# A gated feed-forward kernel: the crossbar copy of x rows 256-511 moves to second place on SyncE's queue, and the first weight slices to ScalarE's

## The chip, the cores and the metric

The kernel runs on one core of one Trainium2 chip. The metric is the device time of one execution in microseconds. The kernel before has a median of 163.7 us over three runs (163.27 to 163.84). A profiled execution, taken apart from these, is where durations and order come from.

## The reference

The kernel computes `(silu(x @ w_gate) * (x @ w_up)) @ w_down` in bf16:

```python
B, S, D, F = 1, 2048, 640, 1536
g = _silu(x @ w_gate)          # x: B, S, D   w_gate: D, F
u = x @ w_up                   # w_up: D, F
return (g * u) @ w_down        # w_down: F, D
```

D is five pieces of 128 rows, F is twelve, S is four blocks of 512 rows.

## The kernel before, in words

TensorE multiplies a stationary tile (loaded by a weight load, shown as PEld) with a moving tile of up to 512 columns and adds up in PSUM. For the first two products the moving tile is x transposed, with D on the partitions: the array `xT`. For each of the four blocks of 512 rows of x and each of the twelve pieces of F, five matmuls over D give the gate sum `pg` and five more the up sum `pu` (line 193). ScalarE applies Silu (line 214), VectorE multiplies (line 215) and writes `aT`. Then twelve matmuls over F for each output tile make the third product (lines 261 and 290), and the outputs are copied and stored. The last four rows of x are computed on VectorE in the gaps (`row_dots`, line 147); the change does not touch them.

`xT` is made in two ways. Rows 0 to 255 are loaded as they are (`x_sb`, line 86, two loads of 128 rows, one by SyncE, one by ScalarE) and transposed by TensorE: five transposes for each 128 rows into PSUM (line 185), the first two into a tile `po_a`, the other three into `po_b`, and a copy of each tile into `xT` (line 190; ScalarE copies `po_a`, VectorE `po_b`). Rows 256 to 511 and all others come by a DMA that transposes on its way, through the crossbar (`turn_x`, line 105). The function is called at line 118 for rows 256 to 511.

Loads go out on two queues in the order of the program. SyncE's queue (SP in the profile) has x rows 0-127, then the gate slices for D pieces 0, 2 and 4 (line 115; each is 128 rows of D by the first 512 columns of F, 128 KB), then the crossbar copy of x rows 256-511, then the up weights for the first four F pieces (line 83, two loads), then the remaining weights, further crossbar copies, and later the outputs. ScalarE's queue (ACT) has x rows 128-255, then the gate slices for D pieces 1 and 3; after that ScalarE loads its function table and runs one tiny Silu (line 119).

`head()` (from line 219) writes the order of TensorE's work by hand, up to the first four F pieces of the first block; `keep_order` holds the instructions of an engine to the order written. First 18 small matmuls on ones (`warm`, line 176) that need no load, then the transposes of x rows 0-127 and 128-255, and then the gate sums of four F pieces side by side (`EARLY = 4`), each in its own PSUM tile of 512 columns. The list `steps` sets the order: for D piece 0 columns 0-127, then 128-255; for D pieces 1 to 4 columns 0-255; then for all five D pieces columns 256-511, which need the crossbar copy. Each step is four matmuls, one for each F piece, so 44 in all. Then follow the up sums of the same four F pieces with 512 columns at once, and the regular loop.

The flag `start` of a matmul makes it overwrite what stood in the tile instead of adding. The kernel before sets it for D piece 0 at column 0 and again at column 256.

Of the kernel before, what the change touches and what calls it, by code (L numbers as in the profile page):

```python
# [10 lines left out]
def _body(  # L11
# [8 lines left out]
    nc = tc.nc  # L20
# [12 lines left out]
    KD = D // P  # L33
    KF = F // P
    S_BLK = 512
    NSB = S // S_BLK
    SUB = S_BLK // P
    HALF = S_BLK // 2
# [3 lines left out]
    T = 4  # L42
    WT_STEP = 4
    ROW_J = 0
    EARLY = 4
    W_CHUNKS = [(4, 8), (8, 12)]
    assert D % P == 0 and F % P == 0 and S % S_BLK == 0 and D > DA and SUB == 4

# [30 lines left out]
    def wslice(a, b):  # L79
        return slice(a * P, b * P)  # L80

    def load_w(eng, dst, src, a, b):
        eng.dma_start(out=dst[:, :, wslice(a, b)], in_=src[:, :, wslice(a, b)])

    def load_x(eng, c0, c1):
        eng.dma_start(out=x_sb[:, c0:c1, :], in_=x_v[:, c0:c1, :])
# [11 lines left out]
    def keep_order(engine):  # L98

        traced = [i for i in nc.cur_bb.bb.instructions if i.engine == engine]  # L100
        for a, b in zip(traced, traced[1:]):
            issue_order(a, b)

    def turn_x(r0, r1):
        nc.sync.dma_start_transpose(out=xT[:, :, r0:r1], in_=xt_v[r0:r1])
# [4 lines left out]

    load_x(nc.sync, 0, 1)
    load_x(nc.scalar, 1, 2)
    for kd in range(KD):
        eng = (nc.sync, nc.scalar)[kd % 2]
        eng.dma_start(
            out=wg_sb[:, kd, wslice(0, EARLY)], in_=wg_v[:, kd, wslice(0, EARLY)]
        )
    turn_x(HALF, S_BLK)
    nc.scalar.activation(silu_first[:], ones[:, 0:1], ACT.Silu)  # L119
    for a in range(0, EARLY, 2):  # L120
        load_w(nc.sync, wu_sb, wu_v, a, a + 2)
# [52 lines left out]
    def warm(n):  # L174
        for _ in range(n):
            nc.tensor.matmul(  # L176
                pw[:, 0:P], lhsT=ones[:], rhs=ones[:], start=True, stop=True
            )

    def transpose_chunk(c, parts):  # L180
        c_sl = slice(c * P, (c + 1) * P)
        for copy, tag, k0, k1 in parts:
            pt = psum.tile([P, k1 - k0, P], bf16, tag=tag, name="pt")
            for kd in range(k0, k1):
                nc.tensor.transpose(  # L185
                    out=pt[:, kd - k0, :],
                    in_=x_sb[:, c, kd * P : (kd + 1) * P],
                    identity=ident[:],
                )
            copy(out=xT[:, k0:k1, c_sl], in_=pt[:])  # L190

    def proj_step(ps, w_sb, fc, sb, c0, c1, kd):
        nc.tensor.matmul(  # L193
            ps[:, c0:c1],
            lhsT=w_sb[:, kd, fc * P : (fc + 1) * P],
            rhs=xT[:, kd, sb * S_BLK + c0 : sb * S_BLK + c1],
            start=(kd == 0 and c0 in (0, HALF)),
            stop=(kd == KD - 1),
        )

    def proj(ps, w_sb, fc, sb, c0, c1):
        for kd in range(KD):
            proj_step(ps, w_sb, fc, sb, c0, c1, kd)
# [6 lines left out]
    def gate(pg, pu, sb, fc, n_s):  # L210

        s0 = sb * S_BLK
        sg = work.tile([P, S_BLK], f32, name="sg")
        nc.scalar.activation(sg[:, 0:n_s], pg[:, 0:n_s], ACT.Silu)  # L214
        nc.vector.tensor_tensor(  # L215
            out=aT[:, fc, s0 : s0 + n_s], in0=sg[:, 0:n_s], in1=pu[:, 0:n_s], op=ALU.mult
        )

    def head():
        dve, act = nc.vector.tensor_copy, nc.scalar.copy  # L220
        split = [(act, "po_a", 0, 2), (dve, "po_b", 2, KD)]
        pgs = [
            psum.tile([P, S_BLK], f32, tag="gu", name="pg", bufs=4)
            for _ in range(EARLY)
        ]
        warm(N_WARM)
        for c in range(HALF // P):
            transpose_chunk(c, split)

        steps = [(0, 0, P), (0, P, HALF)]  # L230
        steps += [(kd, 0, HALF) for kd in range(1, KD)]
        steps += [(kd, HALF, S_BLK) for kd in range(KD)]
        for kd, c0, c1 in steps:
            for fc in range(EARLY):
                proj_step(pgs[fc], wg_sb, fc, 0, c0, c1, kd)

        for fc in range(EARLY):
            pu = psum.tile([P, S_BLK], f32, tag=("po_a", "po_b")[fc % 2], name="pu")
            proj(pu, wu_sb, fc, 0, 0, S_BLK)
            gate(pgs[fc], pu, 0, fc, S_BLK)  # L240
        keep_order(mybir.EngineType.PE)
        keep_order(mybir.EngineType.Activation)

    head()
    for sb in range(NSB):
        n_s = S_BLK if sb < NSB - 1 else S_BLK - T
        for fc in range(KF):
            if sb == 0 and fc < EARLY:
                continue
# [10 lines left out]
        for kf in range(KF):  # L260
# [4 lines left out]
                start=(kf == 0),  # L265
# [15 lines left out]
        for j in range(SUB):  # L281
# [5 lines left out]
            for c0, c1, tag in cols:  # L287
                po = psum.tile([P, c1 - c0], f32, tag=tag, name="po_a")
                for kf in range(KF):
# [4 lines left out]
                        start=(kf == 0),  # L294
# [3 lines left out]
                if c1 < D:  # L298
                    nc.scalar.copy(ot[:], po[:])  # L299
                    eng = nc.sync  # L300
                else:
                    nc.vector.tensor_copy(out=ot[:], in_=po[:])  # L302
                    eng = nc.scalar
# [81 lines left out]
def kernel(tc, *args):  # L385
    _body(tc, *args)
    tc.close()
    tc.compile()
    _trim(tc.nc)
# [30 lines left out]
```

## Time and profile before

| What | Value |
|---|---|
| Three timed runs | 163.27, 163.7 (median), 163.84 us |
| Profiled execution | 163.03 us, of it the span from first to last instruction 161.7 us |
| TensorE matmul busy | 158.7 us, 784 instructions |
| Weight loads busy | 77.7 us, 796 instructions |
| VectorE busy | 110.9 us |
| ScalarE busy | 42.5 us |
| Gate sums, line 193 | 258 matmuls, 59.6 us |
| Up sums, line 193 | 239 matmuls, 59.0 us |
| Third product, lines 290 and 261 | 42.4 and 10.3 us |
| Crossbar copy of x rows 256-511 | issued at 1.86 us, 2.13 us of issuing, landed 4.4 us after its start |

Busy times of matmuls overlap one another, because they are pipelined: the distance between two starts says more than the duration of one. A DMA has two times: how long the queue's engine works at issuing it, and how long it takes from the start of the issue until its data has landed. The second is what an engine that waits for the data sees.

### The profile page before, as it was taken

The numbers are of one execution on the slowest core, as the hardware profiler recorded it, in microseconds if no ns is written. First come the engines' busy times: TensorE is split into PE (matmuls) and PEld (weight loads), VectorE is DVE, ScalarE is ACT, GpSimd is POOL, SyncE is SP. The second block draws the span as 40 slices with busy tenths as digits, with TensorE's granted clock in tenths as the row PEclk, the third lists the DMA queues.
The fourth block names the chain that finished last, engine by engine and source line by source line (L and its number), as shares of the span: only waits on it lengthen the run. The fifth ranks groups of instructions, "written<-read, shape, count | busy, mean of one in ns | idle before, by whom it ended". The sixth has DMA issues, their size and how long they took to land.

```text
span 161.7 us, 2102 instructions
## 1 busy us (share of the span) xinstructions
PE 158.7 (98%) x784; PEld 77.7 (48%) x796; DVE 110.9 (69%) x249; ACT 42.5 (26%) x74; POOL 0.6 (0%) x6
## 2 busy tenths in 40 slices
PE   9999999999999999999999999999999999999995
PEld 8854444444444444444444444444444444445464
DVE  2035322599479999889919999979955999993000
ACT  5051222112322222211222322221213222222121
POOL 1000000000000000000000000000000000000000
PEclk9999999999999999999999999999999999999999
DMA  7999999998199993003110000000321000000312
GB/s 230 257 346 353 363 228 209 231 184 135 34 192 167 201 202 84 4 0 38 61 65 0 0 4 2 0 0 6 59 67 34 0 0 0 0 0 4 54 35 73
DMA packets 41817, 15.86 MB, mean 98 GB/s; under 512 B 33232, under 2 KB 41680, under 8 KB 41808
## 3 DMA queue, kind: packets, MB, share of 16 engines
q1 hardware_dynamic: 33296, 14.78, 38.6%
q10 hardware_dynamic: 8512, 0.95, 3.9%
q8 instruction: 6, 0.10, 0.3%
q14 instruction: 3, 0.02, 0.1%
HBM read 6.88 MB, written 2.62 MB: 59 GB/s over the span
## 4 chain that ended last, share of the span: by engine, by line
PE 98%; issue 1%; DVE 0%
PE pg L193 32%; PE pu L193 32%; PE po_a L290 26%; PE po_t L261 6%; PE pw L176 1%; PE pt L185 1%; DVE ot_b L302 0%; DVE ones L109 0%
## 5 line engine op out<-in xcount | busy, mean ns | idle before, releaser
L193 PE MATMUL pg<-xT,wg_sb 128*128 128x512 bf16 (+3 forms) x258 | 59.6, 364 | 0.3
L193 PE MATMUL pu<-xT,wu_sb 128*128 128x512 bf16 (+1 forms) x239 | 59.0, 379 | 0.1
L215 DVE TENSOR_TENSOR aT<-sg,pu 128x512 bf16<-128x512 f32 (+1 forms) x48 | 32.8, 682 | 32.3 <-PE pu L193 32.3
L214 ACT ACTIVATE sg<-pg 128x512 f32<-128x512 f32 (+1 forms) x48 | 28.4, 596 | 70.9 <-PE pg L193 65.6
L290 PE MATMUL po_a<-wd_sb,aT 128*128 128x512 bf16 (+2 forms) x212 | 42.4, 358 | 0.2
L147 DVE SCALAR_TENSOR_TENSOR prod<-wgT,x_row 128x640 f32<-128x640 bf16 x48 | 39.4, 820 | 1.2
L147 DVE SCALAR_TENSOR_TENSOR prod<-wuT,x_row 128x640 f32<-128x640 bf16 x48 | 39.4, 821 | 1.0
L193 PEld LDWEIGHTS <-wg_sb 128*128 128x128 bf16 x264 | 26.1, 100 | 26.5
L193 PEld LDWEIGHTS <-wu_sb 128*128 128x128 bf16 x240 | 23.4, 98 | 28.0
L290 PEld LDWEIGHTS <-aT 128*128 128x128 bf16 x216 | 20.7, 98 | 21.7
L299 ACT CAST ot<-po_a 128x512 bf16<-128x512 f32 (+1 forms) x17 | 9.5, 560 | 32.0 <-PE po_a L290 20.7
L261 PE MATMUL po_t<-aT,wd_sb 128*128 128x512 bf16 (+1 forms) x47 | 10.3, 366 | 0.1
L261 PEld LDWEIGHTS <-wd_sb 128*128 128x128 bf16 x48 | 4.7, 98 | 5.1
L302 DVE CAST ot_b<-po_a 128x128 bf16<-128x128 f32 x1 | 0.3, 290 | 9.9 <-PE po_a L290 9.9
L270 ACT CAST ot_t<-po_t 128x512 bf16<-128x512 f32 (+1 forms) x4 | 2.2, 558 | 11.6 <-PE po_t L261 11.6
L147 DVE DVE_READ_ACCUMULATOR prod<-wuT,x_row 128x1 f32 x48 | 3.9, 82 | 0.0
L147 DVE DVE_READ_ACCUMULATOR prod<-wgT,x_row 128x1 f32 x48 | 3.9, 81 | 0.0
L272 DVE STREAM_TRANSPOSE ot_q<-ot_t 128x512 bf16<-128x512 bf16 (+1 forms) x4 | 2.7, 677 | 1.7 <-ACT ot_t L270 1.7
L190 DVE COPY xT<-pt 128x384 bf16<-128x384 bf16 x2 | 0.7, 356 | 3.0 <-PE pt L185 3.0
L176 PE MATMUL pw<-ones 128*128 128x128 bf16 x18 | 2.1, 313 | 0.4 <-DVE ones L109 0.4
L176 PEld LDWEIGHTS <-ones 128*128 128x128 bf16 x18 | 1.8, 148 | 0.4 <-DVE ones L109 0.4
L119 ACT ACT_TABLE_LOAD x1 | 1.3, 1283 | 1.5 <-issue 1.5
(13 smaller groups left out, 4.6 us busy)
## 6 DMA issues: line engine op xcount, KB each, us to landing
wd_sb<-in_w_down_dram SPq DMA_DIRECT2D x1, 1920.0 KB, 13.7
out_dram<-ot SPq DMA_DIRECT2D x15, 128.0 KB, 1.7
wg_sb<-in_w_gate_dram SPq DMA_DIRECT2D x2, 640.0 KB, 7.4
wu_sb<-in_w_up_dram SPq DMA_DIRECT2D x2, 640.0 KB, 8.4
wu_sb<-in_w_up_dram SPq DMA_DIRECT2D x2, 320.0 KB, 4.4
x_row<-in_x_dram SPq DMA_DIRECT2D x1, 640.0 KB, 5.4
wg_sb<-in_w_gate_dram SPq DMA_DIRECT2D x3, 128.0 KB, 3.7
out_dram<-ot_q ACTq DMA_DIRECT2D x12, 32.0 KB, 1.9
```

The lines of the kernel that those rows point to most:

```text
L119: nc.scalar.activation(silu_first[:], ones[:, 0:1], ACT.Silu)
L147: nc.vector.scalar_tensor_tensor(out=prod[:], in0=wT[:, fc, :], scalar=1.0, in1=x_row[:, t, :], op0=ALU.mult, op1=ALU.mult, accum_out=acc[ ...
L176: nc.tensor.matmul(pw[:, 0:P], lhsT=ones[:], rhs=ones[:], start=True, stop=True)
L185: nc.tensor.transpose(out=pt[:, kd - k0, :], in_=x_sb[:, c, kd * P : (kd + 1) * P], identity=ident[:],)
L193: nc.tensor.matmul(ps[:, c0:c1], lhsT=w_sb[:, kd, fc * P : (fc + 1) * P], rhs=xT[:, kd, sb * S_BLK + c0 : sb * S_BLK + c1], start=(kd == 0 ...
L214: nc.scalar.activation(sg[:, 0:n_s], pg[:, 0:n_s], ACT.Silu)
L215: nc.vector.tensor_tensor(out=aT[:, fc, s0 : s0 + n_s], in0=sg[:, 0:n_s], in1=pu[:, 0:n_s], op=ALU.mult)
L261: nc.tensor.matmul(po_t[:], lhsT=wd_sb[:, kf, DA:D], rhs=aT[:, kf, sb * S_BLK : sb * S_BLK + n_t], start=(kf == 0), stop=(kf == KF - 1),)
L270: nc.scalar.copy(ot_t[:], po_t[:])
L272: nc.vector.transpose(out=ot_q[:], in_=ot_t[:])
L290: nc.tensor.matmul(po[:], lhsT=aT[:, kf, s0 : s0 + P], rhs=wd_sb[:, kf, c0:c1], start=(kf == 0), stop=(kf == KF - 1),)
L299: nc.scalar.copy(ot[:], po[:])
```

## The change

The crossbar copy of x rows 256-511 is issued by SyncE directly after x rows 0-127. The gate slices for D pieces 0, 1 and 2 are issued by ScalarE, those for D pieces 3 and 4 by SyncE, after the crossbar copy. The steps of the head are: D piece 0 in two parts and D pieces 1 and 2 on columns 0-255; D pieces 0, 1, 2 on columns 256-511; D pieces 3 and 4 on all 512 columns. That is 36 matmuls instead of 44, over the same columns. The flag `start` is set at column 0 alone, since a second one at column 256 would fall into the middle of a sum that goes on over all 512 columns. VectorE makes all four copies of transposed tiles; ScalarE makes none.

```diff
-    EARLY = 4
+    EARLY, STEPS = 4, 3
...
     load_x(nc.sync, 0, 1)
     load_x(nc.scalar, 1, 2)
+    turn_x(HALF, S_BLK)
     for kd in range(KD):
-        eng = (nc.sync, nc.scalar)[kd % 2]
+        eng = nc.scalar if kd < STEPS else nc.sync
         eng.dma_start(
             out=wg_sb[:, kd, wslice(0, EARLY)], in_=wg_v[:, kd, wslice(0, EARLY)]
         )
-    turn_x(HALF, S_BLK)
     nc.scalar.activation(silu_first[:], ones[:, 0:1], ACT.Silu)
...
-            start=(kd == 0 and c0 in (0, HALF)),
+            start=(kd == 0 and c0 == 0),
...
-        dve, act = nc.vector.tensor_copy, nc.scalar.copy
-        split = [(act, "po_a", 0, 2), (dve, "po_b", 2, KD)]
+        copy = nc.vector.tensor_copy
+        split = [(copy, "po_a", 0, 2), (copy, "po_b", 2, KD)]
...
         steps = [(0, 0, P), (0, P, HALF)]
-        steps += [(kd, 0, HALF) for kd in range(1, KD)]
-        steps += [(kd, HALF, S_BLK) for kd in range(KD)]
+        steps += [(kd, 0, HALF) for kd in range(1, STEPS)]
+        steps += [(kd, HALF, S_BLK) for kd in range(STEPS)]
+        steps += [(kd, 0, S_BLK) for kd in range(STEPS, KD)]
```

## The prediction

> I name the five weight slices of the first gate matmuls, one per 128-row piece of D, D0 to D4; "the copy" is the crossbar copy of x rows 256-511 (line 105, called at line 118).
>
> **What bounds the kernel now.** First the busy times and the chain of work that ended last, on the page:
>
> ```profile
> PE 158.7 (98%) x784; PEld 77.7 (48%) x796; DVE 110.9 (69%) x249; ACT 42.5 (26%) x74; POOL 0.6 (0%) x6
> ...
> PE 98%; issue 1%; DVE 0%
> ```
>
> TensorE is the whole chain. A change of queues can then gain only where TensorE waits, and lose only where it makes it wait. The diff touches the head, so next comes the chain of the first 14 us, in order of time (start, us, what):
>
> ```profile
> 0.39 2.10 PE pw L176 x18
> 2.50 1.12 PE pt L185 x10
> 3.62 5.14 PE pg L193 x44
> 8.76 0.22 PE pu L193
> ```
>
> Eighteen warm-up matmuls, ten transposes and 44 gate pieces follow each other without a wait. Then the timeline of the same stretch (start, us, engine; the lines with q are a queue's issues):
>
> ```profile
> 0.00 0.39 SPq L86 DMA_DIRECT2D x_sb<-in_x_dram  x1
> 0.13 0.39 ACTq L86 DMA_DIRECT2D x_sb<-in_x_dram  x1
> ...
> 0.45 1.36 SPq L115 DMA_DIRECT2D wg_sb<-in_w_gate_dram  x3
> 0.55 0.93 ACTq L115 DMA_DIRECT2D wg_sb<-in_w_gate_dram  x2
> ...
> 1.51 1.28 ACT L119 ACT_TABLE_LOAD   x1 [1.51 <-issue]
> 1.86 2.13 SPq L105 DMA_TRANSPOSE xT<-in_x_dram  x1
> ...
> 3.30 5.17 PEld L193 LDWEIGHTS <-wg_sb 128*128 128x128 bf16 x44
> 3.41 5.35 PE L193 MATMUL pg<-xT,wg_sb 128*128 128x128 bf16 x44
> ...
> 4.03 1.15 SPq L83 DMA_DIRECT2D wu_sb<-in_w_up_dram  x2
> ```
>
> With the time to landing that the view by source gives for each issue, this makes a table of margins. D0 (SP, 0.45+2.8) lands at 3.25 and its weight load starts at 3.30. D1 (ACT, 0.55+3.5) lands at 4.05, its load starts at 4.16. D2 (SP, 0.91+3.7): 4.6, used at 4.9. D3 (ACT, 1.03+3.8): 4.8, used at 5.43. D4 (SP, 1.38+3.7): 5.05, used at 5.86. The copy (1.86+4.4): 6.25, used at 6.41. Everything arrives just in time and nothing late: there is no stall for the change to remove.
>
> One more thing is read from spacing. The 256-column pieces start 0.21 us apart until 4.90 (at 4.69, then at 4.90), and from 5.10 to 8.59 there are 32 pieces, 0.109 us each. TensorE's clock doubles near 5.08, after 4.7 us without a gap. (The granted-clock column shows 1.00 in every window from 0 on, so it does not show this; the spacing does.)
>
> **The change part by part**, in the time of the profiled execution: span 161.7 us, execution 163.03 us. The three timed runs have a median of 163.7, 0.67 more; I add the difference that I work out to this median.
>
> 1. *Sixteen 256-column pieces (D3, D4) become eight of 512.* At full clock 2 x 0.109 against 0.216 (five pieces of 512 columns in 1.08 us on the chain): 8 x 0.002, a gain of 0.02 us. Pieces that would have run at half clock gain nothing.
>
> 2. *Copies of the transposed chunks, all on VectorE.* Before, ScalarE's two of 128x256 take 0.36 us each and VectorE's two of 128x384 0.36. On VectorE alone the first can start when its transposes end, near 2.8 instead of 2.91, and the four run one after another. A 256-column copy on VectorE is not shown: between 0.24 (0.356 by columns) and 0.36. The third then ends at 3.7 to 3.85, for a piece that starts at 3.83 today; the fourth at 4.1 to 4.2, for D2. Cost 0 to 0.03 us, and 0 if D0 is late (next step). ScalarE must lose these copies, since its third load moves the table load from 1.51 to about 2.0 and its end to 3.3; the next ScalarE work is the Silu at 8.47.
>
> 3. *D0 moves to ScalarE's second place.* This is the step that counts. That place is D1's today: issued at 0.55 behind the same x rows 128-255 on the same queue, landed 3.5 us later. So D0 at 4.05 instead of 3.25, for a load that wants to start at 3.30: a gap of 0.7 to 0.75 us in TensorE. Lower end: it lands as SP's D0 did, 0.55+2.8 = 3.35, a gap of 0.05. Upper end from the only rows where ScalarE's transfers start beside a crossbar copy in flight (stores of line 274; the first answer is for 34 to 37 us, the second for 70 to 160):
>
> ```profile
> DMA to landing us min/median/max: 3.1/3.4/3.5
> ```
>
> ```profile
> DMA to landing us min/median/max: 1.6/1.9/1.9
> ```
>
> Beside the copy of wgT (issued 31.87 to 35.54) they took 1.6 us longer: 4.05+1.6 = 5.65, a gap of 2.3. I take 0.7, the row of the same queue, place and size; there it competes with SP's ordinary loads instead of the copy. [...]
>
> 4. *D1, D2 in ScalarE's third and fourth place.* D1 as today's D3: 1.03+3.8 = 4.8, needed when D0's eight pieces (0.107 each) end at 4.95. D2, issued at about 1.5, as today's D4 by 3.7: 5.2, needed at 5.4 or later. No further gap at the middle; behind the copy they slip with D0.
>
> 5. *The copy as SP's second load.* Issued at 0.45 instead of 1.86: 4.85, needed after D2's first half, 5.9. It is 1 us early where it was 0.16 us early. Nothing is gained, since nothing waited. Its issue holds SP for 2.13 us, so D3 and D4 are issued at about 2.6 and 3.0. By the fastest and the slowest delay of the slices and the copy (2.8, 4.4) they land between 5.4 and 7.4; D3 is needed near 7.2, D4 near 8.05. Line 83's loads go out 0.5 us sooner than at 4.03, because SP issues one load fewer ahead of them, while TensorE is later: every later margin grows.
>
> **What the gap costs.** If the clock still doubles at 5.08, the gap removes 0.7 us of half-clock work, which is made up at full clock: 0.35 us. If the doubling comes later by the gap, 0.7 us. I take the middle, 0.5, with the 0.02 of step 1 inside its rounding. **163.7 + 0.5 = 164.2 us** (163.5 by the profiled execution). Own range of this case: 163.9 to 164.5.
>
> **Rivals.**
>
> A. *No gap.* The copy's packets start late (SP works 2.13 us at issuing it) and leave the 16 engines to ScalarE's queue until then. For: x rows 0-127 are then the only other load ahead of it. Against: step 3's rows. Time 163.6 to 163.9.
>
> B. *The copy shuts ScalarE's queue out.* For: the stores at 34.5. Against: those came when the copy was nearly all issued, D0 comes 0.1 us after its start. Decides if D0 lands after 4.6. Gap 1.3 to 2.3 us, cost 0.65 to 2.3: 164.4 to 166.0.
>
> C. *The gap costs the clock.* The doubling came after 4.7 us of gapless work. If D0's gap starts this count anew at 4.1, the clock doubles at 8.8. Half-clock work from 4.1 to 8.8 is worth 2.35 us at full clock; before did 0.83+3.7 = 4.55 in the same time (from 3.41). Loss 2.2: 165.9. For: the only rise in the trace followed gapless work. Against: a gap of 0.7 in 4.7 leaves TensorE 85% busy, and no row shows what share is needed. [...]
>
> D. *Faster.* If in most executions the clock doubles well before 5.08, before is held by arrivals: an earlier rise could gain it only the 0.16 us that the copy has in hand, while after, with its copy at 4.85, could keep up to 0.5 more. For: the three runs differ by 0.57 us although the program is the same. Against: the profiled execution, the fastest of the four, shows no arrival that held TensorE, so late arrivals are not shown to be what the others lose. It decides if D0 also comes by 3.5. Time 163.2.
>
> **Numbers.** About 0.3% (0.49 us) is what a measurement of this kernel can tell from no change. Forecast 0.40 (0.28 of it over that bound, 0.12 within it), A 0.15, B 0.12, C 0.15, D 0.18 (0.15 over the bound, 0.03 within). Slower 0.28+0.12+0.15 = 0.55, within 0.12+0.15+0.03 = 0.30, faster 0.15. Cases of both signs hold weight, so the range reaches from D's 163.2 to C's 165.9; only B's far end and what lies beyond D are left out.
>
> **What would show it.** Right: TensorE's first weight load of wg_sb near 4.1 with idle time before it that a load ended; D0's time to landing 3.5; the copy landed by 4.9 and nobody waiting for it; spacing 0.109 from about 5.1 to 5.8. A: first gate piece at 3.4. B: D0 to landing over 4.1, x rows 128-255 perhaps late too. C: spacing 0.21 until 8 us. D: fast spacing before 4.5 us. I am wrong in kind if a wait shows at line 83's loads, at D3 or D4, or at a copy on VectorE, which I hold for covered.

## The result, and the profile after

The changed kernel takes 167.79 us (median of six runs, 166.48 to 168.78); the kernel before, beside it, 163.62 us (163.12 to 163.84). The ratio is 1.0254, with a 95% interval of 1.0218 to 1.0291: slower by about 4.2 us, where 0.5 was forecast and 165.9 was the upper end of the range. Each ratio below is to the kernel before timed beside that run (medians of 163.48 to 163.59 us). The ratios of the runs e5, e10 and e11 below leave out executions more than 1.5% above the fastest of their kernel, while their medians hold all.

The profiled execution of the changed kernel took 166.76 us, span 165.4 against 161.7. The up sums of the head start at 12.35 us instead of 8.59, 3.76 us later, and that is the whole difference of the spans. The chain of the first 14 us, which was TensorE alone before (start, us, what):

```profile
...
1.03 5.80 DMA wg_sb<-in_w_gate_dram
6.83 0.05 issue
6.87 5.64 PE pg L193 x28
12.51 1.51 PE pu L193 x7
```

A load is on the chain now: the second of ScalarE's three slices, D1. It is issued at 1.03 and lands 5.8 us later, at 6.83, where step 4 had 3.8. In the timeline, idle time ahead of a row stands in brackets, with what ended it:

```profile
0.46 2.03 SPq L105 DMA_TRANSPOSE xT<-in_x_dram  x1
0.55 1.41 ACTq L116 DMA_DIRECT2D wg_sb<-in_w_gate_dram  x3
...
3.85 0.62 PE L193 MATMUL pg<-xT,wg_sb 128*128 128x128 bf16 x8 [0.34 <-DMA wg_sb<-in_w_gate_dram]
...
6.87 5.64 PE L193 MATMUL pg<-xT,wg_sb 128*128 128x256 bf16 x28 [2.40 <-DMA wg_sb<-in_w_gate_dram]
```

D0's gap is 0.34 us, less than the 0.7 forecast: D0 landed 3.3 us after its issue. The gap that was not forecast is the next one, 2.40 us ahead of D1. The copy of x rows 256-511, which landed 4.4 us after its issue before, now takes 7.0.

A second loss follows from the gap. The view by windows shows the granted clock (the column after POOL); the first three numbers are a stretch's start and end and its length, then comes TensorE's busy time:

```profile
3.27:6.68 3.41, 0.86 (x12) 0.51 (x9) 0.66 (x3) 0.21 (x2) 0.00 (x0) 1.00 1.14 177
6.68:10.09 3.41, 3.22 (x16) 2.30 (x17) 0.00 (x0) 0.00 (x0) 0.00 (x0) 0.50 1.17 306
10.09:12.35 2.26, 2.26 (x15) 1.26 (x13) 0.00 (x0) 0.45 (x1) 0.00 (x0) 1.00 1.10 347
```

Full clock came early, at 3.27 (from there D0's pieces are 0.056 us apart instead of 0.107), was lost at 6.68, with 0.86 us of TensorE work in the 3.41 us between, and was back at 10.09. All work from 6.87 to 10.09 ran at half clock (0.50 in the second line), 3.2 us that would take 1.6 at full clock.

The sum for the profiled execution, from starts of pieces: waits of 0.46 and 2.56, together 3.0; plus 1.6 for the second half-clock stretch; less 0.8, because the kernel before did its gate pieces from 3.41 to 5.08 at half clock, and here the same pieces ran at full clock or are counted in the second half-clock stretch. That makes 3.8, against 3.76 measured.

### The profile page after: what moved, and what is told of

Read it like the earlier page. It is cut to its first block, busy times and chain, and to the rows that moved or that the text cites. A ratio compares the mean times of both kernels' runs of the same rounds, so it can differ in the third digit from the quotient of the medians.

```text
span 165.4 us, 2098 instructions
## 1 busy us (share of the span) xinstructions
PE 160.3 (97%) x788; PEld 77.1 (47%) x788; DVE 111.2 (67%) x251; ACT 41.9 (25%) x72; POOL 0.6 (0%) x6
## 4 chain that ended last, share of the span: by engine, by line
PE 95%; DMA 4%; ACTq 1%; DVE 0%; issue 0%
PE pg L193 32%; PE pu L193 31%; PE po_a L291 25%; PE po_t L262 6%; DMA wg_sb<-in_w_gate_dram 4%; ACTq L116 0%; ACTq L86 0%; DVE ot_b L303 0%
## 5 line engine op out<-in xcount | busy, mean ns | idle before, releaser
L193 PE MATMUL pg<-xT,wg_sb 128*128 128x512 bf16 (+3 forms) x256 | 60.8, 374 | 2.7 <-DMA wg_sb<-in_w_gate_dram 2.7
L193 PEld LDWEIGHTS <-wg_sb 128*128 128x128 bf16 x256 | 25.4, 101 | 30.6 <-DMA wg_sb<-in_w_gate_dram 3.1
L190 DVE COPY xT<-pt 128x256 bf16<-128x256 bf16 (+1 forms) x4 | 1.1, 318 | 2.5 <-PE pt L185 2.5
```

The source lines that it names most:

```text
L193: nc.tensor.matmul(ps[:, c0:c1], lhsT=w_sb[:, kd, fc * P : (fc + 1) * P], rhs=xT[:, kd, sb * S_BLK + c0 : sb * S_BLK + c1], start=(kd == 0 ...
```

## The experiments

Theory M: the crossbar copy and ScalarE's slices, in flight together, slow each other. Rivals: Q, ScalarE's queue is slow by itself; B, any 327 KB in the copy's place make the slices late; S, a copy issued this early is slow by itself; and theory C on how much of the loss is the clock. (B here, any bytes, is not rival B of the prediction, the crossbar copy shutting ScalarE's queue out.)

### e1: the copy behind the slices again

```diff
-    turn_x(HALF, S_BLK)
     for kd in range(KD):
         ...
+    turn_x(HALF, S_BLK)
```

> The changed kernel with the crossbar copy issued by SyncE after D3 and D4 again; queues of the slices, steps and copies as changed. Theory M (mixing: the copy's 256-byte packets and ScalarE's slices slow each other while both are in flight): D0 lands near 3.3 to 3.6, D1 by 4.3, D2 by 4.8, the copy by 6.3 as before; the gap of 2.4 us ahead of D1 goes. A wait of up to 0.9 us for the copy stays, since the new steps want it at 5.4. Time 163.6 to 164.8. Theory Q (ScalarE's queue is slow by itself when it carries three slices behind x rows): D1 still lands after 5.5 and the time stays above 166.

164.57 us, ratio 1.0066 (1.0041 to 1.0092). The gap ahead of D1 is gone, and about three quarters of the loss with it; the copy landed at 6.73. Theory Q falls: D1 landed at 5.19, and the time is far below 166. But M's landing times fail too: D0 landed 4.1 us after its issue, D1 4.2, D2 4.1, so D0 came at 4.6 and not at 3.3 to 3.6. TensorE's longest wait was 0.70 us, for D0:

```profile
4.66 6.41 PE L193 MATMUL pg<-xT,wg_sb 128*128 128x128 bf16 x36 [0.70 <-DMA wg_sb<-in_w_gate_dram]
```

The place of the copy is most of the loss. What is left shows in this profile (of the slowest of the six executions) as the wait for D0, which comes later from its place on ScalarE's queue than from SyncE's (3.25 us in the kernel before). The new steps have a share too, as e6 and e10 below show.

### e2 and e3: no copy, and an ordinary load of the same bytes

```diff
 # e2
-    turn_x(HALF, S_BLK)
+    nc.vector.memset(xT[:, :, HALF:S_BLK], 0.0)
 # e3
-    turn_x(HALF, S_BLK)
+    x_more = consts.tile([P, 2, D], bf16)
+    nc.sync.dma_start(out=x_more[:], in_=x_v[:, 2:4, :])
+    nc.vector.memset(xT[:, :, HALF:S_BLK], 0.0)
```

> The changed kernel without the crossbar copy of x rows 256-511: VectorE fills these columns of xT with zeros, so the outputs of these rows are not computed from x. Theory M, and theory B (any 327 KB ahead of or beside the slices make them late): D0 by 3.5, D1 by 4.1, D2 by 4.6, no gap in TensorE over 0.3 us, time 162.9 to 163.8. Theory Q: D1 after 5.5, time above 166.

> As e2 (x rows 256-511 of xT are zeros), but in the copy's place SyncE issues an ordinary load of the same 327 KB of x (1280-byte rows) that nothing reads. Theory M (the crossbar's packets): D1 lands by 4.7, D2 by 5.2, time 163.0 to 164.2. Theory B (the bytes): D1 lands after 5.5, a gap of over 1.2 us ahead of it, time above 165.5.

e2: 164.94 us, 1.0102 (1.0039 to 1.0165). e3: 165.44 us, 1.0121 (1.0069 to 1.0174). Neither theory was right on both. In e2, without any copy, D1 still landed 4.6 us after its issue, at 5.59, and D2 at 6.54: SyncE's queue, relieved of the copy, put its up loads (320 KB each, the first issued at 1.39) beside ScalarE's slices. So e2 does not remove the competition, it changes it. In e3, D0 to D2 took 4.0, 4.4 and 4.5 us; TensorE waited 0.87 us ahead of D0 and hardly after it. So e3 misses M clearly and B narrowly (D1 landed at 5.46, B had after 5.5 and a gap ahead of it). B's mechanism is real in part: with ordinary bytes in the copy's place the kernel is still 2.0 us slower than before, about half of the loss with the copy. How late they make a single slice is not sharp: D1 takes 4.4 here, 4.2 in e1 and 3.8 in e10, against 5.8 with the copy. What the crossbar adds shows in the DMA view from 3.0 to 5.5 us (packets, MB and mean rate; then the two queues), of the changed kernel

```profile
DMA packets 1080, 0.35 MB, mean 142 GB/s; under 512 B 976, under 2 KB 1080, under 8 KB 1080
...
q1 hardware_dynamic: 966, 0.25, 90.1%
q10 hardware_dynamic: 114, 0.11, 33.3%
```

and of e3:

```profile
DMA packets 1030, 0.88 MB, mean 352 GB/s; under 512 B 96, under 2 KB 1030, under 8 KB 1030
...
q1 hardware_dynamic: 602, 0.49, 61.2%
q10 hardware_dynamic: 428, 0.39, 45.3%
```

q1 is SyncE's queue, q10 ScalarE's. By the shares the engines are busy in both (123% and 107%, both queues together), but with the copy on q1 they move 142 GB/s instead of 352. ScalarE's queue is not shut out: it gets 0.11 MB through, and each of its 1 KB packets takes longer (33.3% for 114 packets, against 45.3% for 428; of 16 engines over 2.5 us that is 117 ns a packet, against 42).

The copy is slowed as well; by itself it is faster. In the kernel before it hardly met ScalarE's slices, although it was issued at 1.86: from 3 to 4 us the DMA view has only 40 packets under 512 B, from 4.0 to 4.5 us it has 307 and 0.01 MB on ScalarE's queue, and after that the copy is alone. From 4.5 to 5.5 us:

```profile
DMA packets 943, 0.24 MB, mean 240 GB/s; under 512 B 943, under 2 KB 943, under 8 KB 943
...
q1 hardware_dynamic: 943, 0.24, 123.8%
```

That is 21 ns for a packet of the copy, against 37 in the changed kernel (90.1% for 966 packets). So both kinds of packets take longer where they meet, 1.8 times for the copy's and 2.8 times for ScalarE's. These figures come from single executions, but they do not hang on landing times. The last of x, slices and the 327 KB landed at 6.0 us in e3 and at 8.0 in the changed kernel.

### e4: matmuls that fill the gap

```diff
+    N_FILL = 40
...
+        pf = psum.tile([P, P], f32, tag="po_a", name="pf")
         for kd, c0, c1 in steps:
+            for _ in range(N_FILL if (kd, c0) == (1, 0) else 0):
+                nc.tensor.matmul(
+                    pf[:], lhsT=ones[:], rhs=ones[:], start=True, stop=True
+                )
```

> The changed kernel with 40 more matmuls of 128 columns on ones between D0's pieces and D1's (2.2 us at full clock), in a PSUM tile that is free then. D1 still lands near 6.8. Theory C (the idle time itself is 2.7 us of the loss, the clock that falls in it another 1.6): the clock stays at full speed after its first rise, gate pieces of 256 columns are 0.109 apart throughout, time 1.3 to 1.7 us below the changed kernel's, about 166.2. Rival (the clock is no matter, arrivals alone set the end): no change, 167.8.

165.55 us, 1.014 (1.0106 to 1.0173), 2.2 us below the changed kernel, more than the 1.3 to 1.7 forecast. D1 took 6.0 us and landed at 7.02, no earlier than in the changed kernel (the copy took 7.1), and the clock, once up at 5.40, stayed up. So by the medians about half of the 4.2 us is the clock: work in the gap that computes nothing takes this half away, while every load is as late as it was. The two profiled executions give less, 1.2 us between their first up sums (12.35 and 11.19): 1.6 at half clock, less the 0.4 by which D1's pieces start later in e4 (7.28), where the added matmuls end after D1 has landed. The slower executions of the changed kernel, up to 168.78 us, are in no profile.

### e5: the slices behind the copy on one queue

```diff
-        eng = nc.scalar if kd < STEPS else nc.sync
+        eng = nc.sync
```

> The changed kernel with all five slices behind the crossbar copy on SyncE's queue, none on ScalarE's: the same bytes, but nothing is mixed with the copy except the end of x rows 128-255. Theory M (mixing slows both): the copy lands by 5.0 instead of 7.45, D0 near 5.3, the last slice by 7.4 instead of 8.0; one gap of about 2 us ahead of D0 and no further one over 0.5 us; time 165.5 to 167.3, the clock paying as in the changed kernel. Theory S (a crossbar copy issued this early is slow by itself): the copy lands after 6.8 as in the changed kernel, D0 after 7, time above 168.

165.68 us (163.86 to 166.62 in ten runs), ratio 1.0093 (1.0054 to 1.0132). In its profile the copy took 3.9 us from issue to landing instead of 7.0 and landed at 4.32; D0 landed at 5.20 and the last slice at 7.11 instead of 8.02. The same bytes in the same order of need, but one after the other, and the copy is nearly twice as fast: M holds, S falls. D0 comes later than in the changed kernel (3.81), the last slice sooner. The edit changes two things, the queue of the slices and the time of their issue (from 2.11 us on instead of 0.55); no run separates them. The clock, up at 3.49, stayed up in this execution, which at 164.00 us is one of four at 164.3 and below; the other six are at 165.6 and above, and no profile shows what they lose. TensorE waited once:

```profile
5.24 4.53 PE L193 MATMUL pg<-xT,wg_sb 128*128 128x128 bf16 x36 [1.55 <-DMA wg_sb<-in_w_gate_dram]
```

The DMA view of the same stretch as above, all on one queue:

```profile
DMA packets 1172, 0.61 MB, mean 245 GB/s; under 512 B 739, under 2 KB 1172, under 8 KB 1172
```

### e6 and e7: steps alone, VectorE's copies alone

```diff
 # e6, on the kernel before
-            start=(kd == 0 and c0 in (0, HALF)),
+            start=(kd == 0 and c0 == 0),
...
-        steps += [(kd, 0, HALF) for kd in range(1, KD)]
-        steps += [(kd, HALF, S_BLK) for kd in range(KD)]
+        steps += [(kd, 0, HALF) for kd in range(1, STEPS)]
+        steps += [(kd, HALF, S_BLK) for kd in range(STEPS)]
+        steps += [(kd, 0, S_BLK) for kd in range(STEPS, KD)]
 # e7, on the kernel before
-        split = [(act, "po_a", 0, 2), (dve, "po_b", 2, KD)]
+        split = [(copy, "po_a", 0, 2), (copy, "po_b", 2, KD)]
```

> The kernel before with one part of the change: three D pieces on both row halves, then two at 512 columns, flag start at column 0 alone. Queues and copies as before, so the copy still lands at about 6.25, but the steps want it at 5.3 to 5.4: a wait of up to 0.9 us, 164.0 to 165.5 by whether the clock falls for it. Rival (the order of the steps is no matter as long as the queues are as before): 163.3 to 163.8.

> The kernel before with one part of the change: all four copies of transposed tiles on VectorE. The weight slices come later than the copies, so nothing changes: 163.2 to 163.8. Rival (the third and fourth copy are late for D0's second part): 163.9 to 164.3 with a wait of pg for a copy.

e6: 164.25 us, 1.0045 (1.0029 to 1.006): the new steps by themselves cost 0.7 us. The wait for the copy is there, but at 1.17 us it is longer than the 0.9 expected, since the copy landed at 6.79 and not at 6.25:

```profile
6.83 3.20 PE L193 MATMUL pg<-xT,wg_sb 128*128 128x256 bf16 x20 [1.17 <-DMA xT<-in_x_dram]
```

e7: 163.41 us, 0.9994 (0.9981 to 1.0008): the copies on VectorE change nothing.

### e9: the clock alone, without touching a load

```diff
-    N_WARM = 18
+    N_WARM = 9
```

> The kernel before with 9 warm-up matmuls instead of 18; loads untouched. TensorE is idle from 1.35 to 2.36. [...]

163.98 us, 1.0023 (1.0005 to 1.0041): slower by 0.4 us. The author's estimate for a late rise of the clock was 0.8 to 1.7; the sign is right, the size is half of the least. In the profile TensorE is idle for 0.97 us ahead of the transposes, and the clock rises late, at 7.61. The 6.8 us ahead of that rise in two equal parts (columns as above, TensorE's busy time first):

```profile
0.79:4.20 3.41, 2.44 (x23) 2.05 (x22) 0.71 (x2) 2.16 (x4) 0.14 (x1) 1.00 0.93 257
4.20:7.61 3.41, 3.41 (x20) 2.33 (x18) 0.00 (x0) 0.00 (x0) 0.00 (x0) 1.00 1.23 235
```

(The granted-clock column starts with the first record and cannot be read before it; spacing shows half clock until 7.61.) Why the loss is only 0.4 is not settled. The next run suggests one reason: where the clock rises early, the kernel before waits for loads, so that an early rise is worth less to it.

### e0: the kernel before, profiled again

> The kernel before, unchanged, profiled a second time. If the profiled execution that the prediction was read from was a favourable one (its 163.03 us against a median of 163.6), this one shows the copy landing at 6.7 to 7.0 instead of 6.25 and TensorE waiting 0.2 to 0.6 us for it ahead of columns 256-511. Rival (the 0.6 us come from the time of the clock's rise alone): the copy by 6.4, no wait, and the clock rises after 5.5.

163.43 us. The copy landed 4.9 us after its issue, at 6.79, and TensorE waited twice for loads in its gate pieces. By the spacing of the pieces the clock rose near 3.85 us here, not at 5.07:

```profile
5.08 1.51 PE L193 MATMUL pg<-xT,wg_sb 128*128 128x256 bf16 x12 [0.27 <-DMA wg_sb<-in_w_gate_dram]
6.83 2.34 PE L193 MATMUL pg<-xT,wg_sb 128*128 128x256 bf16 x20 [0.24 <-DMA xT<-in_x_dram]
```

The profile that the prediction was read from was a favourable execution. The copy landed at 6.79 and 6.91 in e6 and e7 too, and at 7.02 in e9, whose queues are those of the kernel before.

### e10: the slices' queues alone

```diff
 # on e7
-        eng = (nc.sync, nc.scalar)[kd % 2]
+        eng = nc.scalar if kd < 3 else nc.sync
```

> The kernel before with the copies on VectorE (which e7 shows to cost nothing) and one more part of the change: slices D0 to D2 by ScalarE, D3 and D4 by SyncE, the crossbar copy behind them as before; steps as before. If the queue part costs by itself: D0 at 4.0 to 4.6 instead of 3.3 to 3.6, D1 near 5.2, and 0.5 to 1.2 us more than before, 164.1 to 164.8. Rival (only the copy's place costs): at most 163.8.

163.83 us (163.34 to 165.98 in ten runs), 1.0031 (0.9998 to 1.0064): between the two, and it can't be told from no change by the ratio. In the profile D0, D1, D2 took 3.5, 3.8 and 3.9 us, almost the delays that steps 3 and 4 took from the rows, with a gap of 0.43 ahead of D0. e1 has the same loads in the same order and differs only in the steps, which leaves them 0.7 us between the two medians, as in e6. Its delays of 4.1, 4.2 and 4.1 show that such a delay differs by 0.2 to 0.6 us between executions. Four of the ten runs lie at 165.5 and above, the other six at 164.03 and below; no profile caught one of the four, so a fall of the clock is only a likely reason.

### e11 and e12: two versions with the copy between the slices

```diff
 # on e6; e11 has STEPS = 4, e12 STEPS = 3
     for kd in range(KD):
+        if kd == STEPS:
+            turn_x(HALF, S_BLK)
-        eng = (nc.sync, nc.scalar)[kd % 2]
+        eng = nc.sync if kd >= STEPS else (nc.sync, nc.scalar)[kd % 2]
         ...
-    turn_x(HALF, S_BLK)
```

> A version that the runs point to: the slices D0 to D3 alternate between the queues as before, then the crossbar copy as SyncE's fourth load, then D4; four D pieces on both row halves, D4 at 512 columns. The copy goes out one slice sooner (1.38 instead of 1.86) and is hardly mixed with ScalarE's slices. If the copy's arrival holds the kernel before in most executions: the copy lands 0.3 to 0.5 us sooner and is wanted 0.4 us sooner, D4 is in time, and the time is 163.0 to 163.6. Rival (D3 by ScalarE mixes with the copy and both slow): D3 after 6, time above 164.

> As e11, with three D pieces on both halves: D0 to D2 alternate, then the copy as SyncE's fourth load, then D3 and D4 on SyncE. ScalarE's queue has only D1, so the copy is mixed with nothing. Theory M (unmixed, the copy takes 3.9 us from issue to landing as in e5): it lands at 5.3 to 5.9, is wanted near 5.4 to 5.6, D3 and D4 land by 7.0: 163.0 to 163.7. Rival (the copy waits for the slices' bytes in any place): it lands after 6.3, wait of 0.8 us and more, 164.0 and above.

e11: 163.57 us (162.70 to 165.55), 0.9989 (0.9971 to 1.0007). e12: 163.70 us, 1.0008 (0.9998 to 1.0018). The copy came about 1 us sooner than in e0, at 5.87 and 5.79, but it was wanted sooner too, and TensorE still waited for it (0.47 us in e12). Neither beats the kernel before.

## Why the prediction was wrong, point by point

- **The sign and the first cause were right.** Slices moved to ScalarE come too late and TensorE waits for them. D0's gap was mis-sized, 0.34 us of idle time instead of 0.7, because D0 took 3.3 us and not 3.5.
- **The step that failed is step 4: "D1 as today's D3: 1.03+3.8 = 4.8 ... No further gap at the middle".** D1 took 5.8 us and left a gap of 2.40. The row was taken from a time when ScalarE's slice ran beside SyncE's ordinary loads, and in the changed kernel it runs beside the crossbar copy. Step 3 had said so of its own row, and put a price on it for D0; step 4 let D1 and D2 slip only together with D0. But by the DMA view SyncE's queue, with the copy on it, moved only 10 packets from 2.25 to 2.5 us and 966 from 3.0 to 5.5. By 2.5 us ScalarE's queue had moved 0.25 MB, of which x rows 128-255 are 0.16, so if it moves them in order, most of D0 was through, and D1 and D2 met nearly all of the copy. e4, with the same queues, repeats it (D0 3.3, D1 6.0). With the copy behind the slices D1 takes 3.8 (e10) to 4.2 (e1), so the row is nearly right there; with nothing of another queue beside it the copy takes 3.9 (e5).
- **Step 5 failed in the same way.** The copy was to land 4.4 us after its issue; it took 7.0. The 4.4 was the row of a copy that moved almost alone, behind the slices. The copy's own lateness held nobody up: it landed at 7.45, and its columns come only after the pieces of D1 and D2, at about 8.5.
- **"What the gap costs" failed in kind.** It had one rise of the clock, on time or late. What happened is a fall: the rise came early (3.27), and the gap then lost it for 3.41 us. e4 gives the clock about 2.2 of the 4.2 us by the medians, 1.2 by the profiles. Rival C named the right kind of loss, time at half clock (3.2 us of work here), but only for a rise put off, and by itself; here it came on top of 3 us of waiting.
- **Rival B was wrong in its picture.** ScalarE's queue was not shut out, and D0, the slice that B watched, was early. The price came from both queues slowing each other. (B's 1.6 us is 1.5 by the medians of the two answers, 3.4 and 1.9.) By the DMA view both queues moved data in the same 2.5 us, 0.25 MB on SyncE's and 0.11 on ScalarE's, at 142 GB/s for the copy mixed with slices, against 240 for the copy alone and 352 for ordinary loads mixed.
- **Rival D's premise was met in one execution, and its result was not.** In e0, where the clock rises near 3.85, the kernel before does wait for arrivals, 0.5 us in two places. "There is no stall for the change to remove" was read from one favourable execution. Moving the copy ahead of the slices makes worse what it was to mend.
- **Right: step 2** (e7: the copies cost nothing), and line 83's loads and D3, D4 held nobody up. Step 1's 0.02 us is less than any run here can tell. With the copy in its old place the new steps by themselves cost 0.7 us (e6); the prediction had priced only their matmuls.

How the 4.2 us divide: by the medians e4 gives 2.2 to the clock. e1, with the copy behind the slices, is 3.2 below the changed kernel and 1.1 above the kernel before. These overlap, since the clock falls in the gap that the copy makes, so they can't be added up.

## What to carry to other kernels

A time to landing was read beside what else was in flight: the same crossbar copy took 3.9 us with hardly anything of another queue beside it (e5), 4.4 and 4.9 behind the slices (the kernel before, e0) and 7.0 beside them. So when a DMA is moved, take the rows of its new neighbours for every transfer it will now meet, not for the first one alone. Here the packets of the copy took 37 ns instead of 21 and those of ScalarE's slices 117 instead of 42 where they met, so keep such a copy away from ordinary loads of the other queue that someone is waiting for; one after the other on one queue was faster for the copy and for the last slice (7.11 instead of 8.02, e5), and it cost the first slice 1.4 us. Price a TensorE gap in the head twice, as waiting and as clock (2.40 us and 1.6 us in the changed kernel), and profile the kernel before more than once when the margins in the profile are under 0.2 us.

## What the runs showed of the hardware that was not expected

In two of the profiled executions full clock, once up, was lost again in the head. In the changed kernel the granted clock is 1.00 from 3.27, 0.50 from 6.68 and 1.00 from 10.09 on; the fall lies in TensorE's wait of 2.40 us, which ended at 6.87. In e2 TensorE waited 1.24 us ahead of D1 and 0.34 ahead of D2; the granted clock is 1.00 in the first line and 0.50 in the second, in which TensorE was busy throughout:

```profile
3.36:6.77 3.41, 1.74 (x19) 1.08 (x18) 0.82 (x3) 0.13 (x1) 0.00 (x0) 1.00 0.97 270
6.77:10.18 3.41, 3.41 (x17) 2.31 (x16) 0.00 (x0) 0.00 (x0) 0.00 (x0) 0.50 1.07 352
```

In e5 full clock, up at 3.49, stayed, although TensorE waited 1.55 us. These are single executions, and what decides between the two is not shown by any run here.

The rise, too, comes at different times: at 5.07 in one execution of the kernel before and near 3.85 in the other. The times of the changed kernel spread by 2.3 us, those of the kernel before by 0.7; that the clock makes this difference was not tried.
